# Seven block products instead of eight for the last quarter of the hidden features of a bilinear FFN after memory attention

## Chip, cores and metric

One Trainium2 chip, one of its cores. The metric is the device time of one execution in microseconds (us); the median of the runs is compared.

## What is computed

The reference, cut to what matters (batch 8, 8 heads, 576 tokens, head size 64, 32 memory slots; d_model 512, d_ff 1024):

```python
a = softmax(phi, axis=tokens)
k_m = einsum('bhsm,bhsd->bhmd', a, k);  v_m = einsum('bhsm,bhsd->bhmd', a, v)
attn = softmax(q @ k_m.T / sqrt(64))          # 576 tokens x 32 slots, 8 heads: 576 x 256
x = (attn @ v_m) as 4608 x 512
out = (((x @ w1) * (x @ w2)) @ w3) @ w_out    # 4608 x 512, float32
```

## The kernel before

The kernel folds v_m into w1 and w2: for each batch it makes memory weights of 256 x 1024 for each of the two (256 = 8 heads x 32 slots), and multiplies them by the 256 x 576 attention probabilities. Every large product is made of pieces with a high and a low part (`ah`, `al` of the probabilities, `mh`, `ml` of the memory weights, `sh`, `sl` of g, `Wh`, `Wl` of w3·w_out): three matmuls of 128x128 by 128x288 stand for one product of blocks. Tokens go in two halves n of 288, the 256 slots in two blocks t of 128, the 1024 hidden features f in eight blocks of 128, and w is 0 for a and 1 for b.

One batch has two stages. In the first, 16 units (`ab_unit`, L591, two halves n by eight f) each run 12 matmuls on TensorE into two PSUM banks (L602: two w, two t, three parts), ScalarE copies a to SBUF (L611) and VectorE multiplies b by it into g (L614). In the second, 14 units (`out_unit`, L656) run 12 matmuls each: g times w3·w_out is already done by a seven-product scheme, two units m for each product, in the order 1, 2, 6, 5, 7, 3, 4 (`order`, L638). Each unit wants the high part of its sum of g from ScalarE (`high_part`, L648) and the low part from VectorE (`low_part`, L654, two SBUF inputs). GpSimd (POOL) makes the sums themselves, four steps each: `first_sum` (L620) while g is being made, then S2 and S3 (L632), S1 (L634), S4 (L636). The S2/S3 sums are written into the tile of q, so they wait for the last score matmul (L279) of the next batch. Units 6 and 7 use S1, units 10 and 11 use S4.

Beside this runs the attention of the next batch and the memories of the one after: column maxima and exponentials of phi, the memories (L227, L236), scores (L279), softmax on VectorE (L291 to L319), and the memory weights (L352 on TensorE, high part L363 on ScalarE, low part L371 on VectorE), a quarter q of f at a time.

The order of everything is written out by hand: the strings FIRST, SECOND (batch 1) and BATCH (batch 2 on) are read word by word by `batches` (L728), and each engine keeps that order. `A`, `a`, `g` are the three steps of a unit of the first stage; `O` is a unit of the second stage, `h4`, `l4` its high and low part; `M3`, `Mh3`, `Ml3` the memory weights of quarter 3; `S1` to `S4` and `f0` to `f3` are GpSimd's sums; `sc1`, `scc1`, `mx1`, `sb1`, `ex1`, `sm1`, `mu1`, `tr1`, `ah1`, `al1` are the scores and softmax of the second half of the next batch, `blockc` the copies of the memories. A `-` stands for this batch, `+` for the one after next.

The lines of a unit that the steps below speak of:

```python
for t in range(NT):
    todo += [(mh, ah, t), (mh, al, t), (ml, ah, t)]
...
nc.scalar.copy(out=a_sb, in_=banks[0][:, :HALF])
nc.vector.tensor_tensor(out=G[n, f // half][:, f % half], in0=banks[1][:, :HALF], in1=a_sb, op=ALU.mult)
```

Of the kernel before, what the change touches and what calls it, by code (L numbers as in the profile page):

```python
# [8 lines left out]
F32 = mybir.dt.float32  # L9
F32R = mybir.dt.float32r  # L10
# [5 lines left out]
ALU = mybir.AluOpType  # L16
# [23 lines left out]
A a -mu1 g -M2 -M3 A -Mh2 A -Ml2 a -tr1 -ah1 phi1 g -Mh3 A a -al1 a A kv1 g g top A a -Ml3 a g g A f1 a f0 bm A exp  # L40
bs g A a be g f2 mem a phi2 norm A memc g block +top a blockc g A sc0 kv2 a M1 scc0 g Mh1 M0 mx0 A Mh0 A h0 a Ml1
Ml0 a sb0 +bm ex0 g A +exp +bs a g g sm0 l0 A h1 a A +be O l1 mu0 sc1 h3 +norm a l3 g M2 h2 g scc1 mx1 S2 M3 f3 sb1
S3 Mh2 +mem O h5 Ml2 ex1 S1 l2 h4 +memc l5 l4 S4 O tr0 O p1 h6 C11 Mh3 O ah0 h7 l6 +block sm1 O q2 h10 u2 Ml3 O l7
h8 O h9 l8 h12 l9 mu1 p5 O h11 l10 l12 O al0 l11 h13 tr1 l13 C22 ah1 +blockc O al1 O O O C21 C12
# [14 lines left out]
def memory_attention__then__bilinear_ffn_kernel(  # L59
# [84 lines left out]
    def load_phi(b):  # L144
        t = att.tile([P, NT, S], F32, name="ph", tag="ph")
        nc.sync.dma_start(out=t, in_=phiT[b].rearrange("t p s -> p t s"))
        a = att.tile([P, 9 * P], F32, name="a", tag="a")
        nc.sync.dma_start(out=a, in_=phi_tok[b])
        loaded["ph", b] = t, a

    def load_kv(b):
        t = []
# [26 lines left out]
    def attention(b):  # L179
# [25 lines left out]

        def sub_max():
            ps, n = v["mxb"][0][:, : NT * P], NT * P
            a = v["a"][:, : 4 * n].rearrange("p (c x) -> p c x", c=4)
            nc.vector.tensor_tensor(out=a, in0=a, in1=ps.unsqueeze(1).broadcast_to([P, 4, n]), op=ALU.add)
            for t in range(NT):  # L210
                half = slice(t * D, (t + 1) * D)
                x = v["a"][half, 4 * n :]
                nc.vector.tensor_tensor(out=x, in0=x, in1=ps[half, t * P : (t + 1) * P], op=ALU.add)
            v["mxb"].done(0)
# [128 lines left out]
    def memory_weights(b):  # L343
# [22 lines left out]
        def low(q):  # L366
# [224 lines left out]
    def ab_unit(b, n, f, G):  # L591
# [23 lines left out]
        banks.done(1)  # L615
        yield

    def first_sum(k, G):
        low, top = G[1, 0][:, k], G[0, 0][:, k]
        nc.gpsimd.tensor_tensor(out=low, in0=top, in1=low, op=ALU.subtract)  # L620

    def sums(which, G):

        gp = nc.gpsimd.tensor_tensor
        for k in range(half):
            a, s3, a22, a12 = G[0, 0][:, k], G[1, 0][:, k], G[1, 1][:, k], G[0, 1][:, k]
# [91 lines left out]
    def memory_bank(b, in_a, what):
# [9 lines left out]
    def batches():  # L728
# [7 lines left out]
        for b in range(B):  # L736
            G = {}
            if b:
                room(G)
            ends = ((2, 4, 6, 8), (4, 6, 8))[min(b, 1)]  # L740
            parts = [range(x, y) for x, y in zip((0, *ends), ends)]
            units = [ab_unit(b, n, f, G) for fs in parts for n in range(2) for f in fs]
            ab = {what: iter(units) for what in ("A", "a", "g")}
# [1 line left out]
            for what in tokens((FIRST, SECOND, BATCH)[min(b, 2)]):  # L745
# [98 lines left out]
```

## Time and profile before

| | |
|---|---|
| runs, us | 520.35, 520.26, 520.0 (median 520.26) |
| profiled execution: its time, its span | 520.65, 518.9 |
| granted TensorE clock, mean | 0.999 of 2.4 GHz |
| batches 2 to 5, each | 55.4 to 55.7 us |
| batch 6, batch 7 | 53.3, 51.5 us |
| batch 1 | 61.5 us |

A row of the profile names a line of the kernel, its engine, the operation, the tile written and the tiles read, and its shape; then comes busy time, the mean of one in nanoseconds, and how long the engine stood idle just before, with what ended that. A matmul's 295 ns is the time from its issue to its last result: matmuls overlap, and what one costs in a stream is read from the chain of waits, where a group of them stands with its length. An idle engine other than the one that bounds costs nothing. On VectorE an instruction that follows at once starts some 0.08 us before the one ahead ends, so that its price in a queue is the distance between two starts.

### The profile page before, as it was taken

The numbers are of one execution on the slowest core, as the hardware profiler recorded it, in microseconds if no ns is written. First come the engines' busy times: TensorE is split into PE (matmuls) and PEld (weight loads), VectorE is DVE, ScalarE is ACT, GpSimd is POOL, SyncE is SP. The second block draws the span as 40 slices with busy tenths as digits, with TensorE's granted clock in tenths as the row PEclk, the third lists the DMA queues.
The fourth block names the chain that finished last, engine by engine and source line by source line (L and its number), as shares of the span: only waits on it lengthen the run. The fifth ranks groups of instructions, "written<-read, shape, count | busy, mean of one in ns | idle before, by whom it ended". The sixth has DMA issues, their size and how long they took to land.

```text
span 518.9 us, 11010 instructions
## 1 busy us (share of the span) xinstructions
PE 508.9 (98%) x4488; PEld 443.7 (86%) x4488; DVE 380.6 (73%) x647; ACT 281.1 (54%) x494; POOL 145.7 (28%) x158
## 2 busy tenths in 40 slices
PE   7998999999999999999999999999999999999997
PEld 6344459899888998989988998899898999899996
DVE  4878989889969875778478856885678727982463
ACT  6876989864447635554355625462456334533342
POOL 0005005763011800280025302260118002720280
PEclk9999999999999999999999999999999999999999
DMA  8999943603863138001910084005600320010002
GB/s 276 412 406 358 386 172 108 233 1 124 304 197 110 29 128 302 1 2 51 376 33 1 1 307 151 2 1 196 262 1 1 101 85 1 1 68 24 1 3 91
DMA packets 29795, 68.87 MB, mean 133 GB/s; under 512 B 1840, under 2 KB 10032, under 8 KB 29744
## 3 DMA queue, kind: packets, MB, share of 16 engines
q1 hardware_dynamic: 29744, 68.16, 36.5%
q8 instruction: 35, 0.57, 0.5%
q14 instruction: 16, 0.13, 0.1%
HBM read 58.72 MB, written 9.44 MB: 131 GB/s over the span
## 4 chain that ended last, share of the span: by engine, by line
PE 89%; DMA 6%; DVE 3%; issue 1%; ACT 1%; SPq 0%; ACTq 0%; DVEq 0%
PE ab L602 40%; PE o L670 18%; PE x L670 10%; PE ab L670 5%; PE ab L352 3%; PE x L504 3%; PE x L227 3%; DMA raw<-in_w_out 2%; PE o L504 2%; DMA ph<-in_phiT 2%; PE ab L279 1%; PE o L352 1%; PE x L352 1%; DMA raw<-in_w3T 1%; PE x L279 1%
## 5 line engine op out<-in xcount | busy, mean ns | idle before, releaser
L602 PE MATMUL ab<-ah,mh 128*128 128x288 f32 x512 | 152.7, 298 | 0.0
L602 PE MATMUL ab<-al,mh 128*128 128x288 f32 x512 | 151.0, 295 | 0.0
L602 PE MATMUL ab<-ah,ml 128*128 128x288 f32 x512 | 151.0, 295 | 0.0
L602 PEld LDWEIGHTS ab<-ah,mh 128*128 128x128 f32 x512 | 96.2, 188 | 8.5 <-DVE s_sb L291 3.4
L611 ACT COPY a_sb<-ab 128x288 f32<-128x288 f32 x128 | 50.8, 398 | 94.4 <-PE ab L602 94.2
L614 DVE TENSOR_TENSOR g<-ab,a_sb 128x288 f32<-128x288 f32 x128 | 57.5, 451 | 60.3 <-PE ab L602 59.4
L602 PEld LDWEIGHTS ab<-al,mh 128*128 128x128 f32 x512 | 96.3, 188 | 0.2 <-issue 0.2
L602 PEld LDWEIGHTS ab<-ah,ml 128*128 128x128 f32 x512 | 96.2, 188 | 0.0
L620 POOL TENSOR_TENSOR g<-g,g 128x288 f32<-128x288 f32 x32 | 29.4, 936 | 221.2 <-DVE g L614 221.2
L654 DVE TENSOR_TENSOR sl<-g,sh 128x576 fp32r<-128x576 f32 x98 | 77.6, 813 | 8.7 <-ACT sh L648 8.4
L648 ACT CAST sh<-g 128x576 fp32r<-128x576 f32 x98 | 65.6, 676 | 33.8 <-PE o L670 22.2
L670 PE MATMUL o<-sh,Wh 128*128 128x288 f32 x248 | 73.7, 297 | 0.0
L670 PE MATMUL o<-sl,Wh 128*128 128x288 f32 x248 | 73.2, 295 | 0.0
L670 PE MATMUL o<-sh,Wl 128*128 128x288 f32 x248 | 73.2, 295 | 0.0
L632 POOL TENSOR_TENSOR q<-g,g 128x288 f32<-128x288 f32 x28 | 25.2, 928 | 84.4 <-PE x L279 55.4
L670 PEld LDWEIGHTS o<-sh,Wh 128*128 128x128 f32 x248 | 46.6, 188 | 2.3 <-issue 1.8
L670 PEld LDWEIGHTS o<-sh,Wl 128*128 128x128 f32 x248 | 46.6, 188 | 0.0
L670 PEld LDWEIGHTS o<-sl,Wh 128*128 128x128 f32 x248 | 46.6, 188 | 0.0
L670 PE MATMUL x<-sl,Wh 128*128 128x288 f32 x136 | 40.2, 295 | 0.4 <-DVE sl L654 0.4
L670 PE MATMUL x<-sh,Wh 128*128 128x288 f32 x136 | 40.4, 297 | 0.0
L670 PE MATMUL x<-sh,Wl 128*128 128x288 f32 x136 | 40.1, 295 | 0.0
L636 POOL TENSOR_TENSOR g<-g,q 128x288 f32<-128x288 f32 x28 | 32.3, 1185 | 0.0
(132 smaller groups left out, 886.2 us busy)
## 6 DMA issues: line engine op xcount, KB each, us to landing
kv<-in_kv SPq DMA_DIRECT2D x16, 1024.0 KB, 9.7
q<-in_qT SPq DMA_DIRECT2D x8, 1152.0 KB, 6.2
outT<-c SPq DMA_DIRECT2D x31, 288.0 KB, 2.3
raw<-in_w3T SPq DMA_DIRECT2D x6, 1024.0 KB, 11.5
ph<-in_phiT SPq DMA_DIRECT2D x8, 576.0 KB, 5.4
a<-in_phi_tok SPq DMA_DIRECT2D x8, 576.0 KB, 6.3
raw<-in_w SPq DMA_DIRECT2D x4, 1024.0 KB, 15.5
kv<-in_w SPq DMA_DIRECT2D x3, 1024.0 KB, 14.2
```

Of the source, the lines that this page charges most:

```text
L227: nc.tensor.matmul(ps[t][h * M : (h + 1) * M, : 2 * D], lhsT=v["a"][:, (NT * i + t) * P + h * M : (NT * i + t) * P + (h + 1) * M], rhs=kvt ...
L352: nc.tensor.matmul(ps[t][g * M : (g + 1) * M], lhsT=vm[b % 2][d, g], rhs=w12_sb[q][d, :, g], start=True, stop=True,)
L504: nc.tensor.matmul(pw[r][i][:, cols], lhsT=x[:, i * P : (i + 1) * P], rhs=wos[k // half][:, k % half, cols], start=k == 0 and cols.start == 0,
L602: nc.tensor.matmul(banks[w][:, :HALF], lhsT=x[:, t, w, fc : fc + P], rhs=y[:, n, t * HALF : (t + 1) * HALF], start=i == 0, stop=i == len(t ...
L611: nc.scalar.copy(out=a_sb, in_=banks[0][:, :HALF])
L614: nc.vector.tensor_tensor(out=G[n, f // half][:, f % half], in0=banks[1][:, :HALF], in1=a_sb, op=ALU.mult)
L620: nc.gpsimd.tensor_tensor(out=low, in0=top, in1=low, op=ALU.subtract)
L632: gp(out=s2, in0=a22, in1=s3, op=ALU.subtract)
L636: gp(out=a12, in0=a12, in1=s2, op=ALU.subtract)
L648: nc.scalar.copy(out=hi, in_=src)
L654: nc.vector.tensor_tensor(out=lo, in0=src, in1=hi.bitcast(F32), op=ALU.subtract)
L670: nc.tensor.matmul(ps[j][:, :HALF], lhsT=piece(x, s, 2 * part + k)[:, jc], rhs=y[:, k], start=i in first and part == 0 and k == 0 and t == ...
```

## The change

The probabilities and memory weights of the last quarter (f blocks 6 and 7) are 2 x 2 blocks each: two t by two n, and two t by two f. From batch 2 on (`FIRST_BLOCKS`), their product is made of seven block products P1 to P7 in place of eight, each of six matmuls (two w, three parts). VectorE makes four sums of probabilities in place (T1 to T4), their low parts (Tl), three sums of memory weights (Ms), their low part (Mu); ScalarE makes the high parts (Th, Mt) and a copy (Mr); a difference of weights is made once in batch 1 (Q). Results pass through PSUM: two sums are copied out while the bank goes on accumulating (k, ScalarE), and six sums are finished by VectorE (e), before g (v). The sums of memory weights lie in the tile of q. The scores tile `s_sb` now shares the buffer of `ph`, and `kvm` that of `kv4`. SECOND and BATCH are new orders; FIRST loads phi in two steps (`phi`, `tok`).

```diff
 BATCH = """
-A a g A a g A a A a g phi2 A g +top A a a g g h1 A a +exp +bm A kv2 a f1 sc0 +bs M0 scc0 M1 l1 g mx0 A h0 +be a g
-sb0 A a g g Mh0 A a h2 Ml0 A a A g ex0 sm0 g A a a mu0 A g Mh1 f3 f2 g l2 l0 a g h3 Ml1 tr0 A O sc1 f0 l3 a h8 M2 g
-M3 scc1 mx1 S3 S2 +norm +mem sb1 Mh2 O ex1 Ml2 Mh3 O h4 p1 sm1 O l4 h5 O l5 ah0 S1 +memc h6 l6 mu1 O O h7 l7 u2 O h9
-S4 h10 tr1 l8 l9 O p5 ah1 O l10 Ml3 O h11 l11 +block O C22 h13 l13 C11 h12 l12 C12 q2 al0 O al1 O +blockc C21
+A A a g a g A a -T1 -T3 A g A a g -T2 phi2 -Th1 A +top a g A -Tl1 a g +bm a g tok2 A +exp +bs h0 sc0 scc0 a M0 -T4
+h1 mx0 M1 Mh1 A g A a Mh0 sb0 a g A -Th0 l1 +norm g Ml1 A a a g Ml0 -Tl0 f2 P1 g P2 k10 f0 ex0 k11 l0 P5 k50 sm0 f1
+k51 P6 k20 k21 P3 P7 kv2 e10 O mu0 e11 e20 e40 e21 +be v1 e41 P4 +mem M3 v4 h2 e30 f3 tr0 v2 v3 sc1 Mr Mh3 S2 l2 h4
+Ms M2 S3 O S1 Ml3 h3 O l3 p1 +memc S4 l4 h5 h6 l5 scc1 l6 mx1 O O O h7 l7 O h8 Mt l8 O Mh2 C11 u2 sb1 h9 p5 +block
+h10 Mu q2 h11 l9 l10 ex1 O +blockc l11 O sm1 C22 ah0 h12 l12 h13 O mu1 l13 O O tr1 C12 ah1 al0 O al1 C21 Ml2
 """
...
-                s_sb = att.tile([P, NT * S], F32, name="s_sb")
+                s_sb = att.tile([P, NT, S], F32, name="s_sb", tag="ph")
...
+        def prob_sums(i):
+            (x11, x21), (x12, x22) = [[v["at"][:, n, t * HALF : (t + 1) * HALF] for t in range(NT)] for n in range(2)]
+            out, in0, in1 = {1: (x11, x12, x11), 3: (x12, x22, x12), 2: (x22, x22, x11), 4: (x21, x21, x22)}[i]
+            nc.vector.tensor_tensor(out=out, in0=in0, in1=in1, op=ALU.subtract)
...
+        def block_sums(tmp):
+            p0, p1 = (x.rearrange("p (w f) -> p w f", w=2) for x in ms["ps", NQ - 1][:2])
+            x11, s3, x12, x22 = p0[:, :, :P], p0[:, :, P:], p1[:, :, :P], p1[:, :, P:]
+            if "tmp" not in ms:
+                ms["tmp"] = tmp
+                nc.scalar.copy(out=tmp[:, 0], in_=s3)
+                return
+            for j, x, y, op in ((1, x22, 0, ALU.subtract), (0, x11, 1, ALU.add), (2, x12, 1, ALU.subtract)):
+                nc.vector.tensor_tensor(out=tmp[:, j], in0=x, in1=tmp[:, y], op=op)
...
+    def block_product(b, i, G):
+        (ah, al), (mh, ml), (sh, sl) = ready["A", b], ready["M", b][NQ - 1], ready["M", b]["sums"]
...
+        bank = {2: "beta", 5: "gamma", 3: "gamma"}.get(i, "alpha")
+        if i in (1, 2, 5):
+            G[bank] = pair_x() if i == 2 else pair_ab()
+        for w in range(2):
+            for k, (x, y) in enumerate(((0, 0), (0, 1), (1, 0))):
+                nc.tensor.matmul(
+                    G[bank][w][:, :HALF],
+                    lhsT=xs[x][:, w],
+                    rhs=ys[y],
+                    start=i in (1, 2, 5) and k == 0,
+                    stop=i in (2, 3, 4) and k == 2,
+                    skip_group_check=True,
+                )
...
+    def block_result(i, w, G):
+        if i == 3:
+            G["a_sb"] = big.tile([P, HALF], F32, name="a_sb", bufs=2)
+            nc.scalar.copy(out=G["a_sb"], in_=G["alpha"][0][:, :HALF])
+            G["alpha"].done(0)
+            return
+        bank, kept = {1: ("beta", 1), 2: ("gamma", 2), 4: ("alpha", 5)}[i]
+        c = G["kept", kept][:, w]
+        nc.vector.tensor_tensor(out=c, in0=G[bank][w][:, :HALF], in1=c, op=ALU.add)
...
-            ends = ((2, 4, 6, 8), (4, 6, 8))[min(b, 1)]
+            ends = ((2, 4, 6, 8), (4, 6, 8))[min(b, 1)] if b < FIRST_BLOCKS else (4, 6)
```

The first place where the order matters is TensorE in batch 3, from the last rows of the unit O that stands ahead of the scores to the next unit. Names: `q,km` are the second half's scores, `w_2`, `w_3` the memory weights of quarters 2 and 3, `kv,a` the memories. Before:

```order
L670 MATMUL o<-sl,Wh_82 128x288
L279 MATMUL x<-q,km_74 32x288 x8
L352 MATMUL ab<-w_2_80,vm_76 32x512 x8
L352 MATMUL ab<-w_3_81,vm_76 32x512 x8
L227 MATMUL x<-kv_3080,a 32x128 x8
L227 MATMUL x<-kv_3082,a 32x128 x8
L227 MATMUL x<-kv_3080,a 32x128 x8
L227 MATMUL x<-kv_3082,a 32x128 x8
L236 MATMUL x<-kv_3084,a 32x128 x8
L670 MATMUL o<-sh,Wh_82 128x288
```

Now, with the last block product P4 (its last three rows) between that unit and the memories:

```order
L687 MATMUL ab<-sh,mh_2667 128x288
L687 MATMUL ab<-sl,mh_2667 128x288
L687 MATMUL ab<-sh,ml_2707 128x288
L233 MATMUL x<-kv_3304,a 32x128 x8
L233 MATMUL x<-kv_3306,a 32x128 x8
L233 MATMUL x<-kv_3304,a 32x128 x8
L233 MATMUL x<-kv_3306,a 32x128 x8
L242 MATMUL x<-kv_3308,a 32x128 x8
L377 MATMUL ab<-w_3_81,vm_76 32x512 x8
L284 MATMUL x<-q,km_74 32x288 x8
L377 MATMUL ab<-w_2_80,vm_76 32x512 x8
L771 MATMUL o<-sh,Wh_82 128x288
```

The scores were the first thing behind the unit; now P4, the memories and quarter 3 stand ahead of them, and only quarter 2 behind.

The second place is VectorE in the same batch, from the memory weights' low part after those scores on (`sl` is a low part, `s_sb`, `st`, `ss` the softmax, `c` a result). Before:

```order
L371 TENSOR_TENSOR ml_3411<-ab,mh_3395 128x512 x2
L308 TENSOR_REDUCE ss_3435<-s_sb 128x18
L309 TENSOR_SCALAR ss_3435<-ss_3435 128x18
L310 RECIPROCAL ss_3435<-ss_3435 128x18
L654 TENSOR_TENSOR sl<-q,sh 128x576 x2
L654 TENSOR_TENSOR sl<-g_2930,sh 128x576
L314 TENSOR_TENSOR s_sb<-s_sb,ss_3435 128x576
L654 TENSOR_TENSOR sl<-g_2930,sh 128x576
L319 STREAM_TRANSPOSE at<-s_sb 128x576
L654 TENSOR_TENSOR sl<-g_2932,sh 128x576 x2
```

Now:

```order
L408 TENSOR_TENSOR q<-ab,q 128x256 x3
L396 TENSOR_TENSOR ml_3450<-ab,mh_3410 128x512 x2
L755 TENSOR_TENSOR sl<-g_2960,sh 128x576
L755 TENSOR_TENSOR sl<-q,sh 128x576 x2
L296 STREAM_TRANSPOSE s_sb<-x 128x288 x2
L755 TENSOR_TENSOR sl<-g_2959,sh 128x576
L301 TENSOR_REDUCE st_3492<-s_sb 128x18
L755 TENSOR_TENSOR sl<-g_2959,sh 128x576
L755 TENSOR_TENSOR sl<-g_2961,sh 128x576
L804 TENSOR_TENSOR c<-ab,c 128x288 x2
L305 TENSOR_TENSOR s_sb<-s_sb,st_3492 128x576
L416 TENSOR_TENSOR msl<-q,msh 128x768
```

Three sums (L408) and the low part of them (L416) are added, the low part of unit 3 (`sl<-g_2960`) comes later, and the softmax of the second half is later against the units' low parts.

The third place is GpSimd in batch 1 (`q<-` is S2 and S3). Before, and then now:

```order
L620 TENSOR_TENSOR g_1380<-g_1378,g_1380 128x288 x3
L632 TENSOR_TENSOR q<-g_1381,g_1380 128x288 x2
L620 TENSOR_TENSOR g_1380<-g_1378,g_1380 128x288
L632 TENSOR_TENSOR q<-g_1381,g_1380 128x288 x2
L634 TENSOR_TENSOR g_1378<-q,g_1378 128x288 x4
L636 TENSOR_TENSOR g_1379<-g_1379,q 128x288 x4
```

```order
L722 TENSOR_TENSOR g_1380<-g_1378,g_1380 128x288 x3
L733 TENSOR_TENSOR q<-g_1381,g_1380 128x288 x2
L722 TENSOR_TENSOR g_1380<-g_1378,g_1380 128x288
L733 TENSOR_TENSOR q<-g_1381,g_1380 128x288 x2
L737 TENSOR_TENSOR g_1379<-g_1379,q 128x288 x4
L735 TENSOR_TENSOR g_1378<-q,g_1378 128x288 x4
```

S4 (L737) now stands ahead of S1 (L735).

## Rows read from the trace of the kernel before

**Rows 1.** The page, busy time of each engine, its share of the span, instructions.

```profile
PE 508.9 (98%) x4488; PEld 443.7 (86%) x4488; DVE 380.6 (73%) x647; ACT 281.1 (54%) x494; POOL 145.7 (28%) x158
```

**Rows 2.** Waits of TensorE for VectorE in the second stage: total us, times, longest.

```profile
PE x L670 <- DVE sl L654: 0.4, 1, 0.4
PE ab L670 <- DVE ml L371: 0.3, 1, 0.3
```

**Rows 3.** Stretches of batch 3: length, busy us of each engine, clock, DMA share, GB/s.

```profile
247.75:303.20 55.45, 55.45 (x543) 51.59 (x542) 40.23 (x70) 26.83 (x51) 14.92 (x16) 1.00 0.30 107
...
277.50:301.50 24.00, 24.00 (x276) 22.04 (x276) 19.73 (x32) 12.51 (x22) 11.32 (x12) 1.00 0.08 26
```

**Rows 4.** Chain of waits, batch 3: start us, length us, what.

```profile
247.75 11.11 PE ab L602 x84
...
277.52 0.65 PE x L279 x16
278.17 1.72 PE ab L352 x32
...
282.15 1.79 PE o L670 x12
...
303.20 0.13 PE ab L602
```

**Rows 5.** Timeline of VectorE, batch 3: start, length, instruction, idle before and its end.

```profile
278.28 0.85 DVE L291 STREAM_TRANSPOSE s_sb<-x 128x288 f32<-128x288 f32 x2 [0.42 <-PE x L279]
...
280.02 0.17 DVE L198 RECIPROCAL sm<-sm 128x2 f32<-128x2 f32 x1
280.10 1.21 DVE L300 TENSOR_TENSOR s_sb<-s_sb,st 128x576 f32<-128x576 f32 x1
281.24 1.27 DVE L371 TENSOR_TENSOR ml<-ab,mh 128x512 fp32r<-128x512 f32 x2
...
284.61 1.06 DVE L654 TENSOR_TENSOR sl<-q,sh 128x576 fp32r<-128x576 f32 x1 [0.76 <-ACT sh L648]
...
288.94 1.37 DVE L314 TENSOR_TENSOR s_sb<-s_sb,ss 128x576 f32<-128x576 f32 x1
...
302.08 0.28 DVE L263 TENSOR_SCALAR km<-ab 64x128 f32<-64x128 f32 x1
...
302.88 0.28 DVE L264 COPY vm<-ab 64x128 f32<-64x128 f32 x1
```

**Rows 6.** Timeline of GpSimd, batch 3: the sums S2 and S3, S1, S4.

```profile
278.37 3.61 POOL L632 TENSOR_TENSOR q<-g,g 128x288 f32<-128x288 f32 x4 [11.05 <-PE x L279]
281.94 3.11 POOL L634 TENSOR_TENSOR g<-q,g 128x288 f32<-128x288 f32 x4
285.01 4.68 POOL L636 TENSOR_TENSOR g<-g,q 128x288 f32<-128x288 f32 x4
```

**Rows 7.** Timelines of VectorE and of GpSimd, batch 1.

```profile
172.79 2.71 DVE L654 TENSOR_TENSOR sl<-q,sh 128x576 fp32r<-128x576 f32 x2 [1.40 <-ACT sh L648]
...
172.02 4.15 POOL L634 TENSOR_TENSOR g<-q,g 128x288 f32<-128x288 f32 x4
```

**Rows 8.** Chain of waits, batch 1, where it goes from VectorE back to TensorE.

```profile
180.48 0.68 DVE sl L654
...
181.20 1.59 PE x L670 x10
```

**Rows 9.** The costliest groups, and the durations (min/median/max ns) of VectorE's low parts.

```profile
L611 ACT COPY a_sb<-ab 128x288 f32<-128x288 f32 x128 | 50.8, 398 | 94.4 <-PE ab L602 94.2
L614 DVE TENSOR_TENSOR g<-ab,a_sb 128x288 f32<-128x288 f32 x128 | 57.5, 451 | 60.3 <-PE ab L602 59.4
L648 ACT CAST sh<-g 128x576 fp32r<-128x576 f32 x98 | 65.6, 676 | 33.8 <-PE o L670 22.2
...
L654 DVE TENSOR_TENSOR sl<-g,sh x98: 697/748/1371, 100.0 to 510.7; 128x576 fp32r<-128x576 f32 x98
```

**Rows 10.** DMA issues: what, queue, count, size of one, median us to landing.

```profile
ph<-in_phiT SPq DMA_DIRECT2D x8, 576.0 KB, 5.4
```

More of the change, by code (lines that the diff above doesn't have):

```diff
@@ L41 @@
[L41 to L44, printed above, removed]
+A A tok1 -M2 a -mu1 -tr1 g -M3 phi1 a -Mh3 A g a -ah1 g -al1 -Mh2 A kv1 -Ml3 A a g A a top bm g exp A a bs a A Q
@@ L168, in load_q @@
         loaded["q", b] = t
-    LOADS = {"phi": load_phi, "kv": load_kv, "q": load_q}
+    LOADS = {"phi": load_phi, "tok": load_tok, "kv": load_kv, "q": load_q}
     def load(what, b):
@@ L337, in attention @@
             steps |= {f"{name}{n}": lambda bank, f=f, n=n: f(n) for n in range(2)}
+        steps |= {f"T{i}": lambda bank, i=i: prob_sums(i) for i in range(1, 5)}
+        steps |= {f"Th{n}": lambda bank, n=n: sums_high(n) for n in range(2)}
+        steps |= {f"Tl{n}": lambda bank, n=n: sums_low(n) for n in range(2)}
         return steps
@@ L373, in low, with block_high, block_low @@
             ms[q].append(ml)
+        def block_sums(tmp):
[7 more added lines that the diff above has]
+                nc.vector.tensor_tensor(out=tmp[:, j], in0=x, in1=tmp[:, y], op=op)
+        def block_high():
+            ms["sums"] = [big.tile([P, 3, 2, P], F32R, name=f"ms{x}", tag=f"ms{x}") for x in "hl"]
+            nc.scalar.copy(out=ms["sums"][0], in_=ms["tmp"])
+        def block_low():
+            hi, lo = ms["sums"]
+            nc.vector.tensor_tensor(out=lo, in0=ms["tmp"], in1=hi.bitcast(F32), op=ALU.subtract)
         steps = {f"M{q}": lambda bank, q=q: step(q, bank) for q in range(NQ)}
+        steps |= {x: lambda bank: block_sums(bank()) for x in ("Mr", "Ms")}
+        steps |= {"Mt": lambda bank: block_high(), "Mu": lambda bank: block_low()}
         steps |= {f"Mh{q}": lambda bank, q=q: high(q) for q in range(NQ)}
@@ new lines, in block_keep @@
+    def block_keep(i, w, G):
+        if w == 0:
+            G["kept", i] = big.tile([P, 2, HALF], F32, name="c", tag="c", bufs=3)
+        nc.scalar.copy(out=G["kept", i][:, w], in_=G["gamma" if i == 5 else "alpha"][w][:, :HALF])
+    def block_result(i, w, G):
[7 more added lines that the diff above has]
+        nc.vector.tensor_tensor(out=c, in0=G[bank][w][:, :HALF], in1=c, op=ALU.add)
+        if i == 2:
+            G[bank].done(w)
@@ L618, in first_sum, with block_g @@
+    def block_g(i, G):
+        n, u = (i - 1) % 2, (i - 1) // 2
+        x, y = (G["alpha"][1][:, :HALF], G["a_sb"]) if i == 3 else (G["kept", {1: 1, 2: 2, 4: 5}[i]][:, w] for w in range(2))
+        nc.vector.tensor_tensor(out=G[n, 1][:, half - 2 + u], in0=x, in1=y, op=ALU.mult)
+        if i == 3:
+            G["alpha"].done(1)
     def first_sum(k, G):
@@ L627, in sums @@
             if "S2" not in G:
-                x = att.tile([P, NG, S], F32, name="q", tag="q")
-                G["S2"] = x.rearrange("p g s -> p (g s)")[:, : half * HALF].rearrange("p (k s) -> p k s", k=half)
+                spare(G)
             s2 = G["S2"][:, k]
@@ L707, in memory_attention__then__bilinear_ffn_kernel, with side @@
     n_o = 0
+    def side(b):
+        if b not in beside:
+            beside[b] = pair_x()
+        return beside[b]
     def spare_bank(b, in_a, what):
@@ L712, in spare_bank @@
         if what[0] == "+":
-            return (lambda: beside[b + 1]) if what == "+mem" else pair_x if in_a else pair_ab
+            return (lambda: side(b + 1)) if what == "+mem" else pair_x if in_a else pair_ab
         if what in ("sc0", "sc1") and b:
-            return pair_ab if what == "sc0" else pair_x
+            return pair_ab if what == "sc0" else lambda: side(b + 1)
         return pair_x if in_a else pair_ab
@@ L769, in batches @@
                         steps[at][what.lstrip("-")](memory_bank(b, in_a, what))
+                elif key in ("Mr", "Ms", "Mt", "Mu"):
+                    if b + 1 < B:
+                        steps[b + 1][what](lambda: spare(G))
+                elif key == "P":
+                    block_product(b, int(digit), G)
+                elif key == "k":
+                    block_keep(int(digit[0]), int(digit[1]), G)
+                elif key == "e":
+                    block_result(int(digit[0]), int(digit[1]), G)
+                elif key == "v":
+                    block_g(int(digit), G)
+                elif what == "Q":
+                    x = w12_sb[NQ - 1][D:]
+                    nc.vector.tensor_tensor(out=x[:, :, :, P:], in0=x[:, :, :, :P], in1=x[:, :, :, P:], op=ALU.subtract)
                 elif key == "W":
```

63 lines of the change are left out of this document (47 added, 16 removed).

## Prediction

> **What bounds the kernel now.** I read the page's busy times first [rows 1]: TensorE is busy for 98% of the span, VectorE for 73%. A share of the whole says little, so I went on to the stretches [rows 3]: in batch 3 TensorE is busy for all of its 55.45 us and VectorE for 40.23. The list of waits shows how near VectorE is all the same [rows 2]: in the second stage it made TensorE wait twice, 0.4 and 0.3 us, and the chain of waits shows one of the two, in batch 1, where a low part ends at 181.16 and the matmul that reads it starts at 181.20 [rows 8]. So TensorE's own work is the bound, batch by batch, and the next bound is VectorE between the second half's scores and the next batch's first matmuls. There the stretch from 277.5 to 301.5 has VectorE busy for 19.73 of 24.00 us [rows 3].
>
> **What the change takes away.** A block product is six matmuls (two w, three parts). Eight were 48, seven are 42, so six matmuls go in each of batches 2 to 7, 36 in all. In a stream 84 of them took 11.11 us, 0.1323 us each [rows 4]. That is 0.79 us a batch and 4.76 us in all, on the engine that bounds. The Trainium skill's page "TensorE: Matmul & The Clock Gate", section "Back-to-back issue gap", gives N/2.4 + 2.5 ns for an isolated matmul at full clock, 122.5 ns at 288 columns. By that the sum would start from 4.41 us. The trace does not agree with it, and its 132.3 ns goes into the sum.
>
> **What it adds in the last quarter.** Four sums of probabilities and two low parts on VectorE, and two casts on ScalarE. ScalarE has six PSUM copies of 0.40 us [rows 9] in place of three of its four; VectorE keeps its four products and gets six PSUM sums of about 0.45 us, the price of the product that reads one bank and one tile of SBUF [rows 9]. TensorE must wait where a bank is read and then accumulated again: P6 behind two copies of P1, P7 behind two of P6, P4 behind two sums. Between P1 and P6 stand P2 and P5, 12 matmuls or 1.59 us, against 0.80 us of copies; each w has its own bank, so the first copy starts half a product early. Between P6 and P7 stands P3, 0.79 us, and again half a product. Between P7 and P4 stands a whole unit, 1.59 us. I cost these waits at nothing; that cover gone is a rival below. Copies and sums are the first stage's kind of work, where VectorE idles 59.4 us for TensorE over the kernel [rows 9].
>
> **What it moves, and where that bites: batches 2 to 5.** The last scores now stand behind P4, the memories and quarter 3. GpSimd's S2 writes the tile of q and waits for them [rows 6], and so does ScalarE's copy Mr. From the end of these scores (278.17 in the old trace) to the next batch's second matmul, the one that reads a low part, TensorE now has quarter 2 alone, half of 1.72 us or 0.86, then everything from 282.15 to 303.20 and one matmul more, 21.05 + 0.13 [rows 4]: 22.0 us. The old kernel had 303.33 - 278.17 = 25.2 us there.
>
> What VectorE must do in that time: the 19.73 us of before [rows 3], plus three sums Ms of 256 columns, plus Mu of 768 columns, plus the low part of unit 3, plus the four copies of the memories, 302.08 to 303.16 or 1.1 us [rows 5], less quarter 2's low part, 1.27 us, which now stands behind, and less two small steps of 0.17 us [rows 5], 0.3 us. No row has Ms or Mu. Ms lies between 0.36 us (the copy of 288 columns, scaled by 256/288) and 0.45 us (the product of 288 [rows 9]); I take 0.40, 1.2 us for three. Mu lies between 0.75 us, the median low part of 576 columns [rows 9], and 1.37, the longest such row shown [rows 5]; I take 1.0, in proportion to columns. Sum: 19.73 + 1.2 + 1.0 + 0.75 + 1.1 - 1.27 - 0.3 = 22.2 us. It can't begin at once: the copy Mr needs the scores' end, 0.1 us, and 0.4 us itself [rows 5, 9], so 22.7 us. That is 0.7 us more than TensorE's 22.0, so TensorE waits 0.7 us a batch, first for the low part of unit 9, finally for that of the next batch's probabilities.
>
> **The term that decides: VectorE beside GpSimd.** The 19.73 us holds waits already. While GpSimd works from 278.37 to 289.69 [rows 6], VectorE's steps with two SBUF inputs take 1.21, 1.06 and 1.37 us [rows 5] instead of 0.75; at least 1.4 us is lost so. Two low parts in a row beside S1 took 2.71 us, and S1 itself 4.15 instead of 3.11 us [rows 6, 7]: they take turns. The Trainium skill's page "SBUF — State Buffer", section "Who interferes with whom", states that a VectorE instruction with two SBUF inputs and a GpSimd instruction that reads SBUF block each other for a whole instruction. The rows agree. For the sum I keep the loss of before. Nothing excludes less: bounds are 0 and, if each of the eight remaining sums of GpSimd (0.78 us each, 6.2 us) has to pass ahead of a low part except beside some 2.4 us of one-input work, 3.8 us, which is 2.4 more than before. So the wait lies between 0 and 3.1 us a batch.
>
> **Batches 6, 7 and 1.** Batch 6 has no memories behind it, so 1.1 us of copies is missing in VectorE's sum and the end is on time; I leave the 0.3 us that it waited before [rows 2]. Batch 7 has no attention: it keeps its 0.79 us. Batch 1 pays without gaining. Its VectorE gets Ms, Mu and the difference Q, and its GpSimd does S4 ahead of S1. From the last scores to unit 6's low part TensorE has quarters 2 and 3, 1.72, unit 1, 1.79, four units of 1.59 and two matmuls, 10.1 us [rows 4]. GpSimd must do eleven steps before S1's second is done, 8.6 us, held up by two low parts, some 1.1 us; then a cast, 0.68, and a low part, 0.75 [rows 9]: 11.1 to 11.8 us, the latter with one more turn at the port. That is a wait of 1.0 to 1.7 us, and VectorE, some 0.6 us further behind at unit 7, brings it to 2.0; 0.4 of it stood there before [rows 2], so 1.6 us net, between 0 and 3. Phi of batch 2 now waits for batch 1's scores to leave its buffer; its 5.4 us [rows 10] then end close to where TensorE transposes the maxima. I count it into the 3. The queue that issues it holds the loads of k and v behind it, which are wanted later still.
>
> **The sum**, against the profiled execution's 520.65 us: -4.76 + 4 x 0.7 + 1.6 = -0.36. The median of the runs is 0.39 below that execution, so I put the change on 520.26: 519.9 us. About 0.2% (1.04 us) is what a measurement of this kernel tells from no change.
>
> **The rivals.**
> (a) VectorE's lead holds: GpSimd's sums fall beside one-input work, no waits in batches 2 to 5, and 0.5 us in batch 1. For it: five batches of the old trace have no such wait. Against it: 3.2 us less time there, and more work. 520.26 - 4.76 + 0.5 = 516.0 us.
> (b) The port decides: the low parts now stand one behind the other while GpSimd works, and each loses its turn more often. With 1.0 us more per batch, under half of what the bounds allow, batches 2 to 5 wait 1.7 us each, batch 6 0.6 and batch 1 2.0: 520.26 - 4.76 + 6.8 + 0.6 + 2.0 = 524.9 us, slower. It decides from a wait of 0.8 us per batch on, where 4 x 0.8 + 1.6 has eaten the 4.76. For it speaks the 2.71 us of two neighbours [rows 7]. The skill's page on SBUF would have it so.
> (c) The last quarter isn't covered: the sums ahead of P4 are held up on VectorE behind the softmax of the first half, 0.5 us in six batches: 519.9 + 3.0 = 522.9 us. Against it: a unit of 1.59 us stands between.
> That the change doesn't do what it says is out: TensorE's order has the 42 matmuls.
>
> **Chances.** Forecast, 517.5 to 522.5 us as its own range: 0.45, of which 0.20 falls below 519.2, 0.17 within 0.2% and 0.08 above 521.3. (a) 0.25, all faster. (b) 0.22, all slower. (c) 0.08, 0.03 same and 0.05 slower. So faster 0.45, same 0.20, slower 0.35. The range reaches into (a) and (b) until about 2 in 10 are out: 515.5 to 525.0 us.
>
> **What would show it.** In the profile after: 36 matmuls fewer; batches 2 to 5 within 0.5 us of 55.4; waits of TensorE for low parts of units 9 to 13 and of the probabilities, about 0.7 us a batch; a wait at unit 6 of batch 1; none for the copies of P1 and P6. Batches of 54.7 us would mean (a), of 56 us and more (b). A wait at P4 would be (c). A TensorE wait for a DMA in batch 1 would make me wrong on phi.

## The result, and the profile after

The changed kernel takes 525.05 us (median of four runs, 523.63 to 525.82), the kernel before 520.31: 1.0085 times as long, 95% interval 1.0072 to 1.0098. The profiled execution took 525.82 us with a span of 523.8. The forecast was 519.9 in a range of 515.5 to 525.0.

First the page's busy times, then its 40 slices of TensorE and of its granted clock:

```profile
PE 507.9 (97%) x4452; PEld 442.0 (84%) x4452; DVE 421.4 (80%) x744; ACT 298.8 (57%) x536; POOL 150.5 (29%) x158
...
PE   7998999999999799999999999999999999999997
...
PEclk9999999999999799999999999999999999999999
```

Against [rows 1], the 36 matmuls are gone (4488 before, 4452 now), and VectorE has gone from 380.6 to 421.4 us. One slice in the first third, the fourteenth, shows a 7 for TensorE and a 7 for its clock. It holds the stretch from 170 to 183 us, the second stage of batch 1. The list of TensorE's waits says what it waited for in the second stage:

```profile
PE ab L771 <- DVE ml L396: 7.2, 6, 3.1
```

Six waits, one in each of batches 1 to 6, for one thing: the low part of a quarter of the memory weights. It is the first of batch 1 that is 3.1 us long. Where each batch's first matmul stands in the timeline gives the lengths (for batch 7 to the end of the span):

```
            before   after   difference   forecast
to batch 1  130.66  130.32     -0.34          0
batch 1      61.49   66.24     +4.75        +1.6
batch 2      55.44   55.56     +0.12       -0.09
batches 3-5  55.45   55.80     +0.35 each  -0.09 each
batch 6      53.30   53.37     +0.07       -0.79
batch 7      51.67   50.91     -0.76       -0.79
```

The differences add up to 4.9 us, as the spans do (523.8 and 518.9). So nearly all of the loss is in batch 1, and batches 2 to 6 gain nothing.

**Batch 1.** TensorE, then ScalarE and VectorE in the timeline of batch 1 (start, length, instruction, idle before and what ended it):

```profile
171.19 0.29 PE L771 MATMUL o<-sl,Wh 128*128 128x288 f32 x1
174.63 0.61 PE L771 MATMUL ab<-sh,Wh 128*128 128x288 f32 x1 [3.14 <-DVE ml L396]
175.04 0.44 PE L771 MATMUL ab<-sh,Wl 128*128 128x288 f32 x1
175.28 0.44 PE L771 MATMUL ab<-sl,Wh 128*128 128x288 f32 x1
...
168.94 0.37 ACT L405 COPY q<-ab 128x256 f32<-128x256 f32 x1 [4.01 <-PE ab L377]
170.11 0.68 ACT L749 CAST sh<-q 128x576 fp32r<-128x576 f32 x1 [0.80 <-POOL q L733]
170.69 2.04 ACT L388 CAST mh<-ab 128x512 fp32r<-128x512 f32 x4
...
172.76 1.21 DVE L408 TENSOR_TENSOR q<-ab,q 128x256 f32<-128x256 f32 x3 [4.23 <-ACT mh L388]
173.90 1.28 DVE L396 TENSOR_TENSOR ml<-ab,mh 128x512 fp32r<-128x512 f32 x2
```

Unit 1 issues its last matmul at 171.19, unit 2 its first at 174.63. Unit 2 is the one that goes into a pair of the four `ab` banks, and at that point quarters 3 and 2 of the next batch's memory weights hold all four. A bank comes free when VectorE has made the low part from it. The rows show the line in front of that: ScalarE's cast h4, which waits for GpSimd's S2, then the casts of quarters 2 and 3 (2.04 us), then VectorE's three sums Ms (1.21), and only then the low part of quarter 2 that frees unit 2's bank. VectorE stood idle for 4.23 us before Ms. Before the change, the cast of quarter 2 started while the matmuls of the two quarters ran, its low part came right behind, and unit 2 of batch 1 did not wait (the 0.3 us at `ab` in [rows 2] is in batch 6):

```profile
166.43 1.92 PE L352 MATMUL ab<-w,vm 64*32 64x512 f32 x32
...
167.59 1.07 ACT L363 CAST mh<-ab 128x512 fp32r<-128x512 f32 x2 [2.52 <-PE ab L352]
...
169.28 1.27 DVE L371 TENSOR_TENSOR ml<-ab,mh 128x512 fp32r<-128x512 f32 x2
```

The wait is not the whole price. The matmuls behind it stand 0.24 us apart where 0.13 is usual [rows 4]. The stretches show why (PE, PEld, DVE, ACT, POOL busy, then the granted clock):

```profile
172.00:174.00 2.00, 0.00 (x0) 0.00 (x0) 1.20 (x4) 1.84 (x4) 2.00 (x4) 0.88 0.00 0
174.00:176.00 2.00, 1.37 (x6) 1.37 (x7) 2.00 (x5) 0.04 (x1) 2.00 (x3) 0.50 0.00 0
176.00:178.00 2.00, 2.00 (x10) 2.00 (x10) 2.00 (x3) 0.83 (x3) 2.00 (x3) 0.50 0.00 0
178.00:180.00 2.00, 2.00 (x10) 2.00 (x10) 1.75 (x3) 0.42 (x1) 2.00 (x2) 0.50 0.00 0
180.00:182.00 2.00, 2.00 (x16) 2.00 (x15) 1.37 (x4) 0.67 (x1) 0.15 (x1) 0.91 0.00 0
```

TensorE idles, its granted clock falls to 0.50 (1.2 of 2.4 GHz), and it comes back only after 180 us. The whole of batch 1:

```profile
130.32:196.56 66.24, 63.10 (x658) 57.08 (x657) 52.75 (x95) 33.16 (x63) 14.41 (x16) 0.95 0.41 137
```

3.14 us of it TensorE is idle, all of them at unit 2.

**Batch 3**, as an example of batches 2 to 6, in the same manner, with GpSimd last:

```profile
284.43 0.69 PE L284 MATMUL x<-q,km 64*32 64x288 f32 x16
284.92 1.06 PE L377 MATMUL ab<-w,vm 64*32 64x512 f32 x16
...
288.57 0.38 PE L771 MATMUL ab<-sh,Wh 128*128 128x288 f32 x1 [0.80 <-DVE ml L396]
...
285.23 0.37 ACT L405 COPY q<-ab 128x256 f32<-128x256 f32 x1 [3.67 <-PE x L284]
285.50 1.08 ACT L388 CAST mh<-ab 128x512 fp32r<-128x512 f32 x2
...
286.62 1.21 DVE L408 TENSOR_TENSOR q<-ab,q 128x256 f32<-128x256 f32 x3 [3.56 <-ACT mh L388]
287.75 1.28 DVE L396 TENSOR_TENSOR ml<-ab,mh 128x512 fp32r<-128x512 f32 x2
...
285.33 3.10 POOL L733 TENSOR_TENSOR q<-g,g 128x288 f32<-128x288 f32 x4 [15.39 <-PE x L284]
```

The same wait of unit 2, 0.80 us here: the last scores end at 285.1, the copy Mr waits for them (it writes the tile of q), then come the cast of quarter 3, Ms, and the low part that frees the bank. GpSimd's sums wait for the same scores. VectorE begins Ms 1.5 us behind the scores and then has no idle time up to the low part of the next batch's probabilities (in the second stretch below it is busy for 21.55 of 23.20 us). There TensorE is late a second time, by a little that counts as busy: the batch's second matmul, which reads that low part, starts 0.27 us behind the first.

```profile
307.92 0.29 PE L647 MATMUL ab<-ah,mh 128*128 128x288 f32 x1
308.19 0.40 PE L647 MATMUL ab<-al,mh 128*128 128x288 f32 x1
```

The stretches give, for the whole of batch 3 and then from the end of the scores to the next batch's low part:

```profile
252.12:307.92 55.80, 55.00 (x536) 50.94 (x535) 47.12 (x87) 29.70 (x58) 16.00 (x16) 1.00 0.31 107
285.10:308.30 23.20, 22.40 (x180) 21.18 (x161) 21.55 (x36) 13.90 (x26) 12.41 (x12) 1.00 0.24 78
```

### The profile page after: what moved, and what is told of

The parts are those of the page before. It is cut to its first block, busy times and chain, and to the rows that moved or that the text cites. A ratio compares the mean times of both kernels' runs of the same rounds, so it can differ in the third digit from the quotient of the medians.

```text
span 523.8 us, 11136 instructions
## 1 busy us (share of the span) xinstructions
PE 507.9 (97%) x4452; PEld 442.0 (84%) x4452; DVE 421.4 (80%) x744; ACT 298.8 (57%) x536; POOL 150.5 (29%) x158
## 4 chain that ended last, share of the span: by engine, by line
PE 87%; DMA 6%; DVE 3%; ACT 2%; issue 1%; SPq 0%; POOL 0%; ACTq 0%; DVEq 0%
PE ab L647 32%; PE o L771 17%; PE x L771 10%; PE ab L771 6%; PE ab L687 5%; PE x L549 3%; PE x L233 2%; DMA raw<-in_w_out 2%; PE o L549 2%; DMA ph<-in_phiT 2%; PE ab L377 2%; ACT mh L388 1%; DVE q L408 1%; PE o L377 1%; PE x L377 1%
## 5 line engine op out<-in xcount | busy, mean ns | idle before, releaser
L647 PE MATMUL ab<-ah,mh 128*128 128x288 f32 x416 | 124.3, 299 | 0.0
L647 PE MATMUL ab<-al,mh 128*128 128x288 f32 x416 | 123.2, 296 | 0.0
L647 PE MATMUL ab<-ah,ml 128*128 128x288 f32 x416 | 122.7, 295 | 0.0
L755 DVE TENSOR_TENSOR sl<-g,sh 128x576 fp32r<-128x576 f32 x98 | 82.9, 861 | 5.6 <-ACT sh L749 5.3
L647 PEld LDWEIGHTS ab<-ah,mh 128*128 128x128 f32 x416 | 78.2, 188 | 8.2 <-DVE at L338 4.2
L647 PEld LDWEIGHTS ab<-al,mh 128*128 128x128 f32 x416 | 78.2, 188 | 1.1 <-DVE al L333 0.8
L647 PEld LDWEIGHTS ab<-ah,ml 128*128 128x128 f32 x416 | 78.2, 188 | 0.0
L659 DVE TENSOR_TENSOR g<-ab,a_sb 128x288 f32<-128x288 f32 x104 | 47.0, 454 | 37.4 <-PE ab L647 34.7
L656 ACT COPY a_sb<-ab 128x288 f32<-128x288 f32 x104 | 41.3, 399 | 58.0 <-PE ab L647 54.6
L735 POOL TENSOR_TENSOR g<-q,g 128x288 f32<-128x288 f32 x28 | 33.2, 1217 | 0.0
```

The lines of the kernel that those rows point to most:

```text
L647: nc.tensor.matmul(banks[w][:, :HALF], lhsT=x[:, t, w, fc : fc + P], rhs=y[:, n, t * HALF : (t + 1) * HALF], start=i == 0, stop=i == len(t ...
L755: nc.vector.tensor_tensor(out=lo, in0=src, in1=hi.bitcast(F32), op=ALU.subtract)
```

## Experiments

Theory 1 is the bank: what holds TensorE is the chain of casts, sums and low parts to unit 2's banks. Theory 2 is rival (b) and the load that the forecast had on VectorE: its queue beside GpSimd's sums sets the time, so that a wait removed in one place comes back in another. Ratios are to the kernel before, measured on the same chip. The expectations count the wait at unit 2 from start to start of its matmuls, less the usual 0.13 us: 0.96 us where the profile has 0.80 us of idle time.

**Batch 1: the bank's chain on two engines** (`b1_release`)

```diff
-S2 M2 h4 Mh2 f2 O S3 Mh3 Ms p1 S4 S1 h5 Ml2 scc1 l4 O
+S2 M2 Mh2 h4 f2 O S3 Mh3 Ml2 Ms p1 S4 S1 h5 scc1 l4 O
```

> Only batch 1's order is edited: ScalarE's cast of quarter 2 (Mh2) ahead of the cast h4, and VectorE's low part of quarter 2 (Ml2) ahead of the three sums Ms. Theory 1 (bank): output unit 2 waits 3.1 us in batch 1 because quarter 2 holds its PSUM banks until that low part, which stands behind Ms, the casts of quarter 3 and GpSimd's S2. Then the wait at unit 2 falls under 0.3 us, the granted clock stays at 1.00 there, and a smaller wait of 1.0 to 1.7 us shows at unit 6 behind GpSimd's S4: 519.5 to 521.5 us. Theory 2 (port, VectorE's load): VectorE and GpSimd have as much to do as before, so the wait only moves a few units on, 2.5 us or more: 523 to 525 us.

Measured: 523.38 us, 1.0055 (1.0040 to 1.0070). The wait at unit 2 is gone and the clock stays at 1.00, but now unit 4, unit 6 for its high and for its low part, and unit 8 wait:

```profile
174.69 0.41 PE L771 MATMUL o<-sl,Wh 128*128 128x288 f32 x1 [0.57 <-DVE sl L755]
178.17 0.40 PE L771 MATMUL x<-sh,Wh 128*128 128x288 f32 x1 [0.28 <-ACT sh L749]
179.63 0.40 PE L771 MATMUL x<-sl,Wh 128*128 128x288 f32 x1 [0.93 <-DVE sl L755]
183.70 0.40 PE L771 MATMUL o<-sl,Wh 128*128 128x288 f32 x1 [0.34 <-DVE sl L755]
```

Batch 1 falls from 66.24 to 63.77 us. By time this is theory 2's bracket: the bank is the cause of the 3.1 us, and the waits that stand behind it come to 2.1 us.

**The same, one engine** (`b1_ml2_only`: only Ml2 ahead of Ms)

> The changed kernel, and in batch 1 only VectorE's low part of quarter 2 ahead of the three sums Ms; ScalarE's order stays. Theory 1 (bank): unit 2 then waits for the cast of quarter 2, which ends some 1.0 us after the cast h4, and 0.65 us of the low part: 0.8 to 1.2 us instead of 3.1, the granted clock stays 1.00, and the later waits of b1_release (0.4 to 1.1 us at units 4, 6 and 7) show up as there: 523 to 524.3 us. If the sums Ms are not what holds the bank, the wait stays at 3 us and the clock falls: 525 us.

Measured: 523.35 us, 1.0055 (1.0041 to 1.0069). The row of unit 2:

```profile
172.79 0.40 PE L771 MATMUL ab<-sh,Wh 128*128 128x288 f32 x1 [0.58 <-DVE ml L396]
```

So one word of VectorE's order is worth 2.5 us of the 3.1 us wait, and the whole drop of the clock (1.00 in each 2 us from 172 to 182). Nothing is left for ScalarE's order to give: the total is that of `b1_release`.

**GpSimd's order too** (`b1_release_s1`: `b1_release` with `S1 S4` for `S4 S1`)

> As b1_release, and in batch 1 GpSimd does S1 ahead of S4. Theory 1: also the wait at unit 6 goes, batch 1 within 0.5 us of its 61.5 us before: 518.0 to 519.7 us. Theory 2: no better than b1_release.

Measured: 524.30 us, 1.0074 (1.0059 to 1.0089), no better than without it; in the traces batch 1 is 65.04 us for 63.77. The waits at unit 6 went, as expected, but a new one came at unit 8, 2.11 us for a copy by ScalarE. `both_orders`, below, has the same wait, and shows whose it is.

**The last scores early** (`sc1_early`)

```diff
-P4 +mem M3 v4 h2 e30 f3 tr0 v2 v3 sc1 Mr Mh3 S2 l2 h4
-Ms M2 S3 O S1
+P4 sc1 M3 v4 h2 e30 f3 tr0 v2 v3 Mr Mh3 scc1 O S2 l2 h4
+Ms +mem M2 S3 S1
```

(and `scc1` falls away further on).

> Batch 1 as in the changed kernel; from batch 2 on the last scores stand right behind P4 and quarter 3 behind them, then output unit 1, the memories, quarter 2 and output unit 2, so that the copy Mr can begin 3 us sooner and 4 us of TensorE's work more lie between quarter 3 and unit 2. Theory 1: the wait of 0.97 us at unit 2 goes in batches 2 to 6 and nothing takes its place: batches of 54.7 to 54.9 us, 519.5 to 521 us in all. Theory 2: VectorE's load is the same, waits of 0.7 us or more a batch show at the low parts of units 6 to 13 or at the next batch's probabilities: 523.5 to 525.5 us.

Measured: 521.17 us, 1.0016 (1.0006 to 1.0026), ten runs. Batches 3 to 5 take 54.85 us each and TensorE is busy in all of it:

```profile
250.71:305.56 54.85, 54.85 (x536) 50.74 (x535) 47.52 (x87) 29.92 (x58) 16.56 (x16) 1.00 0.31 109
```

VectorE does as much as in the changed kernel (47.52 against 47.12 us) and GpSimd slightly more, and no wait is left in batches 2 to 5 (batch 6 keeps 0.6 us at unit 2). Theory 2 is out as a matter of load; what counts is where in the batch the work may begin. The edit does two things at once: the scores come 3.2 us sooner in the batch, and unit 1 and the memories now lie between quarter 3 and unit 2. No run separates them.

**Both** (`both_orders`: `b1_release_s1` and `sc1_early`)

> The edits of b1_release_s1 and of sc1_early together. Theory 1: the two gains add, 513 to 515.5 us, which is the 4.76 us of the 36 matmuls below the kernel before, or a little more. Theory 2: 521 us or more.

Measured: 519.63 us, 0.9982 (0.9970 to 0.9995), ten runs: a little below the kernel before, by less than the 0.2% that the forecast counted as no change, and short of the expectation, mostly by batch 1 (64.98 us). Unit 8 waits 2.09 us, for the copy u2, by which ScalarE empties the `o` banks that unit 8 goes on accumulating in. The rows of TensorE and of ScalarE:

```profile
184.29 0.61 PE L771 MATMUL o<-sh,Wh 128*128 128x288 f32 x1 [2.09 <-ACT c L788]
...
181.16 0.67 ACT L749 CAST sh<-g 128x576 fp32r<-128x576 f32 x1 [3.99 <-POOL g L737]
181.74 0.83 ACT L412 CAST msh<-q 128x768 fp32r<-128x768 f32 x1
182.47 1.24 ACT L749 CAST sh<-g 128x576 fp32r<-128x576 f32 x2
183.62 0.63 ACT L788 COPY c<-o 128x576 f32<-128x576 f32 x1
```

The cast at 181.16 is h11, which needs S4; with S4 moved back it holds ScalarE for 4 us, and u2 stands behind it. I had moved GpSimd's step and not the cast that follows from it. Here, too, the clock dropped behind the wait (0.55 and 0.60 from 184 to 188). Of the ten runs, five had a mean clock of 1.000 and a median of 518.82 us, five had 0.993 to 0.997 and 520.72. The trace is of one of the second five; if the others lost their clock in the same place, the drop doesn't come each time, and costs 1.9 us when it does.

**Batch 1 mended** (`both_orders_2`: h11 behind h10, l4 ahead of Ms, l7 ahead of Ml3; then `both_orders_3`)

> As both_orders, and in batch 1 three more edits: ScalarE's cast h11, which needs S4, behind the copies u2 and h10 (in both_orders it stood 4 us in front of the copy that TensorE waited 2.1 us for), VectorE's l4 ahead of Ms and l7 ahead of the low part of quarter 3. Theory 1: every wait of batch 1 is under 0.4 us and its length 61.0 to 61.8 us; the clock stays at 1.00; 515.0 to 516.8 us. Theory 2 (VectorE and GpSimd have too much to do in batch 1): a wait of 1.5 us or more shows at another unit, 517.5 us or more.

Measured: 517.93 us, 0.9950 (0.9936 to 0.9963), all five runs at a clock of 1.000. One wait is left in batch 1, at unit 8, and VectorE's rows show it:

```profile
183.31 0.40 PE L771 MATMUL o<-sl,Wh 128*128 128x288 f32 x1 [1.56 <-DVE sl L755]
...
178.96 1.27 DVE L396 TENSOR_TENSOR ml<-ab,mh 128x512 fp32r<-128x512 f32 x2
180.16 0.95 DVE L305 TENSOR_TENSOR s_sb<-s_sb,st 128x576 f32<-128x576 f32 x1
181.03 1.56 DVE L416 TENSOR_TENSOR msl<-q,msh 128x768 fp32r<-128x768 f32 x1
182.51 2.75 DVE L755 TENSOR_TENSOR sl<-g,sh 128x576 fp32r<-128x576 f32 x4
```

The low part of unit 8 is the first of the four at 182.51, behind three steps that TensorE does not wait for at this point. In `both_orders_3` the low part of unit 8 goes ahead of all three, and that of unit 9 ahead of the last two:

```diff
-h7 O Mt O l7 Ml3 O sb1 Mu h8 h9 l8 u2 l9 O h10 O
+h7 O Mt O l7 h8 l8 Ml3 O h9 u2 l9 O sb1 Mu h10 O
```

> As both_orders_2, and in batch 1 VectorE's low parts of units 8 and 9 ahead of the low part of quarter 3, of the subtraction of the maxima (sb1) and of Mu, behind which TensorE waited 1.6 us for the low part of unit 8. Theory 1: batch 1 falls from 62.1 to 60.4 to 60.9 us, no wait above 0.4 us in it, 516.0 to 516.9 us. Theory 2: the wait only moves to another unit, 517.4 us or more.

Measured: 517.04 us, 0.9936 (0.9923 to 0.9948). Batch 1 takes 61.23 us, a little more than expected, and its one wait is 0.45 us long:

```profile
130.74:191.97 61.23, 60.78 (x658) 54.53 (x657) 53.06 (x94) 32.86 (x63) 15.55 (x16) 1.00 0.43 143
```

This version beats both kernels: 3.4 us below the kernel before, of the 4.76 us that the 36 matmuls took.

**GpSimd's S1 and S4 taken away** (`no_s1_s4`; the kernel leaves these sums out, and the units 6, 7, 10 and 11 take the blocks as they are)

```diff
-Ms M2 S3 O S1 Ml3 h3 O l3 p1 +memc S4 l4
+Ms M2 S3 O Ml3 h3 O l3 p1 +memc l4
```

> The changed kernel without GpSimd's sums S1 and S4 from batch 2 on (left out: units 5 and 3 of the output product are made from the unsummed blocks). Theory 1 (bank): in batches 2 to 6 the chain that TensorE waits for runs from the last scores over Mr, the cast, Ms and the low part of quarter 3, with no sum of GpSimd in it, so the wait of 0.96 us at unit 2 stays and batches 3 to 5 stay at 55.7 to 55.85 us: 524.3 to 525.3 us. Theory 2 (port): GpSimd's work after the scores falls from 12.5 to 3.1 us, VectorE's low parts take 0.75 us each, and each of these batches gets 0.7 us shorter or more: under 522.5 us.

Measured: 523.78 us, 1.0064 (1.0050 to 1.0078), between what the two theories expect. Two neighbouring low parts beside S1, and the same two without it (VectorE, the changed kernel first):

```profile
345.53 2.65 DVE L755 TENSOR_TENSOR sl<-q,sh 128x576 fp32r<-128x576 f32 x2
```

```profile
343.77 1.42 DVE L755 TENSOR_TENSOR sl<-q,sh 128x576 fp32r<-128x576 f32 x2
```

So VectorE gets faster, by 2.4 us in the whole batch (44.67 against 47.12), and TensorE's wait at unit 2 stays at 0.80 us. The batch gets shorter by 0.25 us only, 55.55 after 55.80: that is the late start at the probabilities, where the first matmuls now follow one another at the usual 0.13 us.

**Mr in a tile of its own** (`mr_own_tile`)

```diff
-                nc.scalar.copy(out=tmp[:, 0], in_=s3)
+                ms["r"] = big.tile([P, HALF], F32, name="a_sb", bufs=2)[:, : 2 * P].rearrange("p (w f) -> p w f", w=2)
+                nc.scalar.copy(out=ms["r"], in_=s3)
```

(and the first Ms reads it from there).

> The changed kernel, but ScalarE's copy Mr of quarter 3 goes into a tile of its own (the a_sb ring) instead of into the tile of q, so that it no longer waits for the last scores to have read q; nothing else moves. Theory 1 (bank, the chain starting at the last scores): in batches 2 to 6 the chain starts when quarter 3 is done, 0.7 us sooner, and the wait at unit 2 falls from 0.96 to 0.2 to 0.4 us: batches 3 to 5 of 55.0 to 55.25 us, 521 to 522.8 us in all; the 3.1 us of batch 1 stay, where S2 and the casts of the quarters set the end. Theory 2 (port): no engine does less, so batches 3 to 5 stay within 0.2 us of 55.8: 524 us or more.

Measured: 524.95 us, 1.0088 (1.0072 to 1.0103): no gain. The wait at unit 2 did shrink, and another one appeared, at the low part of unit 9:

```profile
288.56 0.37 PE L772 MATMUL ab<-sh,Wh 128*128 128x288 f32 x1 [0.30 <-DVE ml L396]
300.54 0.40 PE L772 MATMUL o<-sl,Wh 128*128 128x288 f32 x1 [0.17 <-DVE sl L756]
```

The batches stay at 55.80 us. Here theory 1 alone falls: there must be a second chain of the same length. VectorE's queue shows it. Ms begins 0.45 us sooner in the batch, but the first low part behind the bank's takes longer beside GpSimd's sums (the changed kernel first):

```profile
288.94 0.87 DVE L755 TENSOR_TENSOR sl<-g,sh 128x576 fp32r<-128x576 f32 x1
```

```profile
288.93 1.36 DVE L756 TENSOR_TENSOR sl<-g,sh 128x576 fp32r<-128x576 f32 x1
```

So the 0.45 us are lost again, and the low part of the next batch's probabilities begins 55.3 us into the batch in both kernels. This second chain goes from the last scores over GpSimd's sums and VectorE's low parts to those probabilities.

**Both taken away** (`mr_own_no_s1_s4`)

> The edits of mr_own_tile and of no_s1_s4 together (from batch 2 on units 5 and 3 are made from the unsummed blocks). Theory 3: from the last scores on two chains of about the same length hold TensorE up, one over Mr, Ms and the low part of quarter 3 to the PSUM banks of unit 2, the other over GpSimd's sums, the port and VectorE's low parts to unit 9 and the next batch's probabilities; each edit alone shortens one of them and gains 0.0 to 0.3 us a batch. Then both edits together gain 0.6 to 0.8 us a batch: a wait of 0.47 us at unit 2, none above 0.15 us behind it, batches 3 to 5 of 55.0 to 55.2 us. If there is one chain only, with the last scores at its start and the bank at its end (theory 1), mr_own_tile should have shown it and these batches stay above 55.4 us.

Measured: 521.19 us, 1.0017 (1.0004 to 1.0029). Batches 3 to 5 take 55.05 us, the wait at unit 2 is 0.30 us, and none follows:

```profile
286.39 0.38 PE L772 MATMUL ab<-sh,Wh 128*128 128x288 f32 x1 [0.30 <-DVE ml L396]
...
305.73:360.79 55.06, 54.76 (x537) 50.93 (x536) 44.73 (x87) 29.79 (x58) 6.68 (x8) 1.00 0.31 108
```

One edit gains 0.0, the other 0.25, both together 0.75 us a batch: two chains, side by side, of almost one length: the bank's, as theory 1 has it, and VectorE's queue beside GpSimd's sums, as theory 2 has it. In the changed kernel both start at the last scores, which fits that `sc1_early` removes both. Totals tell less here: the wait of batch 1, left as it is, cost up to 1.3 us more or less from trace to trace (last section).

## Why the prediction was wrong

The spans differ by +4.9 us where -0.4 was forecast. Of these 5.2 us, 3.1 are in batch 1, 1.5 in batches 2 to 5 and 0.9 in batch 6; the part ahead of batch 1 gives 0.3 back, which is no gain: it lies anywhere from 129.5 to 131.0 us in the traces of the runs above, which all have the same order there.

- **The matmuls** (36 of 0.1323 us): right, 4452 are left. Batch 7 shows the saving by itself, 0.76 us for a forecast of 0.79. In the other batches 0.60 is what it brings at most (55.45 to 54.85 in `sc1_early`, where TensorE never waits in batches 3 to 5): small steps of 0.1 us at each change between the stream's shape and another, of which that order has two more, were not in the sum.
- **The last quarter costs TensorE nothing**: right. No row of after has TensorE wait for the copies k or the sums e. A sum e took 0.45 us, Ms 0.42 and Mu 0.95; the forecast had 0.45, 0.40 and 1.0. Rival (c) did not happen.
- **VectorE's lead in batches 2 to 5**: the mechanism was half right. The forecast had TensorE short by 0.7 us from the last scores on, first at unit 9 and then at the next batch's probabilities. The trace has 0.8 us (22.40 busy in 23.20), but at unit 2, where the step "first for the low part of unit 9" does not look: it counted what VectorE owes the units and not that VectorE's and ScalarE's work on quarter 3 also holds the PSUM banks of unit 2. That the two sizes lie so near is luck. The chain of the forecast is there beside it, VectorE without idle time from Ms to the next batch's probabilities, and with the bank's chain shortened, unit 9 waits at once (`mr_own_tile`). Its terms were off both ways: it begins 1.5 us behind the scores and not 0.5, because Ms waits for the cast of quarter 3 (1.08 us, not in the sum), and holds some 21.5 us of work for 22.2. That the batch became 0.35 us longer where 0.09 less was forecast is 0.35 us more at unit 2 (the starts of its first two matmuls come 1.05 us late, for 0.7) and 0.24 us at the starts of the batch's first matmuls, less 0.17 us for the scores, memories and quarters in their new order (4.46 us for 4.63).
- **Batch 6**, "the end is on time": wrong by 0.86 us. The bank's chain has none of the memory copies in it whose absence was to make that batch short, so it waits at unit 2 like the others.
- **Batch 1**: this is the step that failed most. The forecast walked from the last scores to unit 6 and found 1.6 us net, by GpSimd's S4 ahead of S1. Unit 2, four units sooner, was not looked at, though the order shows `h4 Mh2` on ScalarE and `Ms ... Ml2` on VectorE. There it lost 3.14 us of idle time, and then some 2.3 us by the clock: TensorE is busy for 63.10 us in this batch, and for 60.78 in `both_orders_3`, where the clock stays up. The 1.6 us of the forecast were not far off either: once the wait at unit 2 is gone, unit 6 waits 1.2 us, and batch 1 takes 2.3 us more than before (`b1_release`).
- **Phi of batch 2**: right, no wait of TensorE for a DMA in batch 1.
- **Rival (b), the port, 524.9 us**: near in time, by another way. VectorE does lose time beside GpSimd: the two low parts above took 2.65 us beside S1 and 1.42 without. The Trainium skill's page "SBUF — State Buffer", section "Who interferes with whom", has a VectorE instruction with two SBUF inputs and a GpSimd instruction that reads SBUF contend; the two low parts agree. But without S1 and S4 a batch is only 0.25 us shorter, and 0.75 us where the bank's chain is shortened too, while the rival needed 1.0 us more than the forecast.

The 0.35 for slower rested on three mechanisms, and the wait for a bank was none of them.

## What to carry to other kernels

When a step is put ahead of another in an engine's order, follow what the one behind it releases, PSUM banks as much as results, and look at the very next unit that allocates them. A wait removed without a gain does not mean that the wait was harmless: shorten two suspected chains one by one and then together, and look for the event at which both begin. An edit that moved that event (here the last scores, with other work put behind them) gained 0.95 us a batch; shortening both chains instead gained 0.75.

## What was not expected of the hardware

- A TensorE wait can cost nearly twice its length. Behind waits of 2.1 us and of 3.1 us the granted clock was 0.50 for some 3 to 6 us; behind waits of 0.6 to 1.6 us it stayed at 1.00. One and the same wait did not always cost the same: behind the 3.1 us at unit 2 of batch 1 the clock was down for some 6 us in the changed kernel and in `mr_own_tile` (batch 1 of 66.2 and 66.5 us), and for some 3 us in `sc1_early`, `no_s1_s4` and `mr_own_no_s1_s4` (65.0 to 65.2 us). By the mean clocks it did not fall in every execution either: the four runs of the changed kernel lie between 523.63 us (mean clock 1.000) and 525.82 (0.993), those of `both_orders` in two groups 1.9 us apart.
